# Part A's attention as one running line of steps: a step's sums grouped by tile shape and placed among the next step's scores, block ends deferred

## The chip, the cores and the metric

The kernel runs on one NeuronCore of a Trainium2 chip. Five engines work side by side, each through its own instructions in order: TensorE (PE, the matmul array, which writes to PSUM), VectorE (DVE), ScalarE (ACT), GpSimd (POOL) and SyncE (SP, which issues transfers). They meet through semaphores. The metric is the device time of one execution in microseconds (us); lower is better.

## What is computed

The reference is the forward pass and all gradients of a gated mix of two attentions over 2048 tokens of width 576. Only attention A is touched by the change; it has 32 query heads of width 18 that share one key head and one value head:

```
q = (x @ wq).reshape(B, S, H, Dh)          # H = 32, Dh = 18
k = x @ wk
v = x @ wv
scores = einsum('bhqd,bkd->bhqk', q, k) * Dh ** (-0.5)
p = softmax(scores)
a = einsum('bhqk,bkd->bhqd', p, v) @ wo
_out, _vjp = jax.vjp(_f, A_x, A_wq, ...)   # _f: g * a + (1 - g) * b
_grads = _vjp(grad_out)
```

Its backward pass needs, for each head, the exponentials E of the scores, the products of grad_out with v (called d here), U = d * E, and sums of E and of U over keys (for the output and dq) and over queries (for dk and dv).

## The kernel before

The program goes through attention A (set-up, attention, final products) and then through the stages of attention B. `a_attention` is the part of interest. It loops over 8 groups g of 4 heads. The 4 heads of a group lie at partitions 0, 32, 64 and 96 of one tile.

A group has two parts. **Part 0** keeps keys on the partitions: for each block of 512 queries (4 blocks) it goes over the 16 key tiles, and sums over keys into two PSUM tiles `a_acc0` and `a_acc1`. **Part 1** keeps queries on the partitions: for each block of 512 keys it goes over the 16 query tiles and sums over queries. That makes 8 x 2 x 4 x 16 = 1024 steps. One step is:

- twice `pair`, for two heads each: two score matmuls into `a_s` (all 128 rows and 128 columns of the array; the masked keys `a_kmask` pick the head), two exponentials on ScalarE from `a_s` into `a_E`, two matmuls into `a_d` that use 32 rows each of the array, and one VectorE product `a_U` = `a_d` * `a_E` over both heads;
- four sums of E: in part 0 with `a_evA` or `a_evB` as weights, 64 columns of the array each, in part 1 with `a_dog`, 32 columns each;
- four sums of U: with `a_ku` in part 0 and `a_qtok` in part 1, 32 columns each.

PSUM is full: two one-bank buffers for `a_s`, two two-bank buffers for `a_d`, one bank for each `a_acc`. `a_s` is free again when its exponential has read it, `a_d` when its product has.

After each part 0 block ScalarE and VectorE copy `a_acc` to `a_accs`, TensorE transposes that (eight f32 transposes into an `a_d` buffer), ScalarE copies it to `a_tk`, and VectorE and GpSimd form the output, dq and the normalised gradient in `a_dog`. After each part 1 block VectorE adds `a_acc` to `a_dvacc` and `a_dkacc`. At the start of a group and between its parts `tr16` makes the transposed `a_qtok`, `a_doT` and `a_doaT`, eight transposes to an `a_d` buffer, with a copy on VectorE or ScalarE in turn (`evac`).

The order on each engine is not the order of the code: the tile framework schedules the instructions by its own priorities. On TensorE it mixes the matmuls of neighbouring steps. The loads of a group are issued by SP (`a_qaug`) and by POOL (`a_dog`).

Of the kernel before, what the change touches and what calls it, by code (L numbers as in the profile page):

```python
# [7 lines left out]
ALU = mybir.AluOpType  # L8
AX = mybir.AxisListType
# [20 lines left out]
class Kern:  # L30
# [3 lines left out]
    def __init__(self, tc, T, A_x, A_wq, A_wk, A_wv, A_wo, B_mem0, B_Wq, B_Wk, B_Wv, B_Wo,  # L34
# [18 lines left out]
        self._evac_i = 0  # L53

# [9 lines left out]

    def mm(self, out, lhsT, rhs, start=True, stop=True, tp=None):
        return self.nc.tensor.matmul(out, lhsT, rhs, start=start, stop=stop,  # L66
                                     tile_position=tp, skip_group_check=True)

    def tr(self, out, in_, nrows, tp=None):
        b = in_.base_partition()  # L70
        return self.nc.tensor.transpose(out, in_, self.identB[b:b + nrows, b:b + nrows], tile_position=tp)  # L71
# [1014 lines left out]
    def a_attention(self, keep, sp, pacc, ps):  # L1086


        nc = self.nc
        T, NTT = self.T, self.NTT  # L1090
        self.otok = keep.tile([P, NTT, D], BF16, name="a_otok")
# [3 lines left out]

        def tr16(src_fn, dst):
            for t4 in range(0, NTT, 8):
                pt = ps.tile([P, 8, P], BF16, name="a_d", bufs=2)
                for t in range(8):
                    self.tr(pt[:, t, :], src_fn(t4 + t), P)  # L1100
                self.evac(dst[:, t4 * P:(t4 + 8) * P], pt[:].rearrange("p t c -> p (t c)"))

        srows = [slice(32 * i, 32 * i + 32) for i in range(4)]
        kmask = keep.tile([P, 4, T], BF16, name="a_kmask")
        nc.gpsimd.memset(kmask[:], 0.0)
        for i in range(4):
            nc.vector.tensor_copy(kmask[srows[i], i, :], self.kaug[srows[i], :])  # L1107

        def pair(pr, sl, sr, dl, dr):

            d = ps.tile([P, 2, 512], F32, name="a_d", bufs=2)
            ex = sp.tile([P, 2, 512], BF16, name="a_E", bufs=4)
            for j in range(2):
                s = ps.tile([P, 512], F32, name="a_s", bufs=2)
                self.mm(s[:, :], lhsT=sl(2 * pr + j), rhs=sr(2 * pr + j))
                nc.scalar.activation(ex[:, j, :], s[:, :], ACT.Exp, scale=SCALEA)  # L1116
            for j in range(2):
                r = srows[2 * pr + j]
                self.mm(d[:, j, :], lhsT=dl(r), rhs=dr(r), tp=(r.start, 0))
            u = sp.tile([P, 2, 512], BF16, name="a_U", bufs=4)  # L1120
            nc.vector.tensor_tensor(out=u[:], in0=d[:], in1=ex[:], op=ALU.mult)  # L1121
            return ex, u

        for g in range(8):
# [3 lines left out]
            nc.gpsimd.dma_start(dog[:, :, :], self.do_dram[g])  # L1128
            qtok = sp.tile([P, NTT * P], BF16, name="a_qtok", bufs=1)
            tr16(lambda t: qaug[:, t * P:(t + 1) * P], qtok)  # L1130
            doT = sp.tile([P, T], BF16, name="a_doT", bufs=1)
            tr16(lambda t: dog[:, t, :], doT)
            for qb in range(T // 512):
                qs = slice(qb * 512, qb * 512 + 512)
                acc = [pacc.tile([P, 512], F32, name=f"a_acc{b}", bufs=1) for b in range(2)]
                for kt in range(NTT):
                    ks = slice(kt * P, (kt + 1) * P)
                    Es, Us = zip(*[pair(pr, lambda i: kmask[:, i, ks], lambda i: qaug[:, qs],
                                        lambda r: self.vaugT[r, ks], lambda r: doT[r, qs]) for pr in range(2)])
                    for pr in range(2):  # L1140
                        ev = self.evA if pr == 0 else self.evB
                        for j in range(2):
                            self.mm(acc[pr][64 * j:64 * j + 64, :], lhsT=ev[:, kt, :], rhs=Es[pr][:, j, :],
                                    start=(kt == 0), stop=False, tp=(0, 64 * j))
                    for pr in range(2):
                        for j in range(2):
                            b = 64 * j + (32 if pr == 0 else 0)
                            self.mm(acc[pr][b:b + 32, :], lhsT=self.ku[:, kt, :], rhs=Us[pr][:, j, :],
                                    start=False, stop=(kt == NTT - 1), tp=(0, b))
                accs = sp.tile([P, 2, 512], F32, name="a_accs", bufs=1)  # L1150
                nc.scalar.copy(accs[:, 0, :], acc[0][:, :])
                nc.vector.tensor_copy(accs[:, 1, :], acc[1][:, :])
                pt = ps.tile([P, 2, 4, P], F32, name="a_d", bufs=2)
                for b in range(2):
                    for t in range(4):
                        nc.tensor.transpose(pt[:, b, t, :], accs[:, b, t * P:(t + 1) * P], self.identF[:])
                tk = sp.tile([P, 2, 4, P], F32, name="a_tk", bufs=1)
                nc.scalar.copy(tk[:], pt[:])
                ts = slice(qb * 4, qb * 4 + 4)
                for b in range(2):  # L1160
                    v = tk[:, b].rearrange("p t (j c) -> p t j c", c=64)
                    o0, k1, k2, u0 = (0, 19, 32, 37) if b == 0 else (32, 51, 0, 5)
                    h0 = 4 * g + 2 * b
                    osl = self.otok[:, ts, h0 * DA:(h0 + 2) * DA].rearrange("p t (j e) -> p t j e", e=DA)
                    qsl = self.dqtok[:, ts, h0 * DA:(h0 + 2) * DA].rearrange("p t (j e) -> p t j e", e=DA)
                    dsl = dog[:, ts, 64 * b:64 * b + 64].rearrange("p t (j c) -> p t j c", c=32)
                    rl = sp.tile([P, 4, 2, 1], F32, name="a_rl", bufs=2)
                    nc.vector.reciprocal(rl[:], v[:, :, :, o0 + 18:o0 + 19])
                    nc.gpsimd.tensor_tensor(out=osl, in0=v[:, :, :, o0:o0 + DA], in1=rl[:].to_broadcast([P, 4, 2, DA]),
                                            op=ALU.mult)  # L1170
                    prod = sp.tile([P, 4, 2, DA], F32, name="a_prod", bufs=2)
                    nc.gpsimd.tensor_tensor(out=prod[:], in0=osl, in1=dsl[:, :, :, 0:DA], op=ALU.mult)
                    dd = sp.tile([P, 4, 2, 1], F32, name="a_dd", bufs=2)
                    nc.vector.tensor_reduce(out=dd[:], in_=prod[:], axis=AX.X, op=ALU.add)
                    m1 = sp.tile([P, 4, 2, DA], F32, name="a_m1", bufs=2)
                    nc.gpsimd.tensor_tensor(out=m1[:, :, :, 0:13], in0=v[:, :, :, k1:k1 + 13],
                                            in1=dd[:].to_broadcast([P, 4, 2, 13]), op=ALU.mult)
                    nc.gpsimd.tensor_tensor(out=m1[:, :, :, 13:18], in0=v[:, :, :, k2:k2 + 5],
                                            in1=dd[:].to_broadcast([P, 4, 2, 5]), op=ALU.mult)
                    nc.gpsimd.tensor_tensor(out=m1[:], in0=v[:, :, :, u0:u0 + DA], in1=m1[:], op=ALU.subtract)  # L1180
                    nc.gpsimd.tensor_tensor(out=dsl[:, :, :, 0:DA], in0=dsl[:, :, :, 0:DA],
                                            in1=rl[:].to_broadcast([P, 4, 2, DA]), op=ALU.mult)
                    nc.vector.scalar_tensor_tensor(out=dsl[:, :, :, DA:DA + 1].rearrange("p t j c -> p t (j c)"),
                                                   in0=dd[:].rearrange("p t j c -> p t (j c)"), scalar=-1.0,
                                                   in1=rl[:].rearrange("p t j c -> p t (j c)"),
                                                   op0=ALU.mult, op1=ALU.mult)
                    rls = sp.tile([P, 4, 2, 1], F32, name="a_rls", bufs=2)
                    nc.gpsimd.tensor_scalar(out=rls[:], in0=rl[:], scalar1=SCALEA, scalar2=None, op0=ALU.mult)
                    nc.gpsimd.tensor_tensor(out=qsl, in0=m1[:], in1=rls[:].to_broadcast([P, 4, 2, DA]), op=ALU.mult)
            doaT = sp.tile([P, T], BF16, name="a_doaT", bufs=1)  # L1190
            tr16(lambda t: dog[:, t, :], doaT)
            for kb in range(T // 512):
                ks = slice(kb * 512, kb * 512 + 512)
                acc = [pacc.tile([P, 512], F32, name=f"a_acc{b}", bufs=1) for b in range(2)]
                for qt in range(NTT):
                    qs = slice(qt * P, (qt + 1) * P)
                    Es, Us = zip(*[pair(pr, lambda i: qaug[:, qs], lambda i: kmask[:, i, ks],
# [227 lines left out]
```

## Time and profile before

| | |
|---|---|
| median of 3 runs | 10380.04 us (10369.47 to 10390.74) |
| profiled execution | 10379.87 us, its span 10378.1 us |
| mean granted TensorE clock | 0.918 |
| PE, DVE, ACT, POOL busy | 9786.8, 4400.1, 3878.9, 1258.1 us |
| first score matmul of the attention | at 188.8 us |
| last sum of the attention | at 3734.3 us |

The span is the time between the first and the last instruction that the profiler saw. PE is busy by the modelled ends of pipelined matmuls, so 94% busy doesn't mean that the array streams 94% of the time: what a matmul costs is read from the distance between starts. In rows of the timeline "x2" merges instructions of one form that overlap or follow at once; the second number is the time from the first start to the last end. A row of a group ends with its busy time, the mean ns of one, and the idle time of its engine just before, with what ended it.

### The profile page before, as it was taken

The page shows a single profiled execution, that of the slowest core. Times are in us where ns is not written, and L with a number is a line of the kernel's source. Part 1 is how long each engine was busy: PE and PEld are TensorE (multiplying, and loading weights), DVE is VectorE, ACT ScalarE, POOL GpSimd, SP SyncE. Part 2 cuts the span into 40 slices and gives each one's busy share as a digit, 9 for nine tenths or more (in the row PEclk, how much of TensorE's full clock was granted, in tenths as well). Part 3 has the DMA queues.
Part 4 walks back from the last instruction along what each step waited for, and adds up shares of the span by engine and source line. Part 5 has one row for each costly group of instructions (what it writes and reads, how often), then busy time and mean ns, then how long its engine had stood idle before and what let it go on. Part 6 is the DMA issues. An engine that isn't in the chain of part 4 may idle for free. (4 is left out here: it accounts for less than half of the span.)

```text
span 10378.1 us, 211015 instructions
## 1 busy us (share of the span) xinstructions
PE 9786.8 (94%) x91222; PEld 4483.1 (43%) x91222; DVE 4400.1 (42%) x6058; ACT 3878.9 (37%) x6906; POOL 1258.1 (12%) x2895
## 2 busy tenths in 40 slices
PE   7999999999999989979999888888799989999899
PEld 2222222222222234435555555555566664555444
DVE  4777777777777744422222333333222221112100
ACT  3667676666766643321121222222111111112100
POOL 3000000000000003310000222322000001112100
PEclk9999999999999999979999877777899997777899
DMA  2000000000000025541111444444422236666644
GB/s 75 1 5 1 5 5 1 5 1 5 5 1 1 1 80 228 235 159 51 49 50 50 168 156 160 159 158 150 147 82 78 77 103 207 187 186 187 199 149 141
DMA packets 550264, 961.40 MB, mean 93 GB/s; under 512 B 183433, under 2 KB 361746, under 8 KB 529170
## 3 DMA queue, kind: packets, MB, share of 16 engines
q1 hardware_dynamic: 482850, 693.21, 20.9%
q0 software_dynamic: 65168, 253.37, 6.5%
q8 instruction: 713, 11.68, 0.5%
q14 instruction: 221, 1.81, 0.1%
q10 hardware_dynamic: 1312, 1.33, 0.0%
HBM read 543.67 MB, written 404.03 MB: 91 GB/s over the span
## 5 line engine op out<-in xcount | busy, mean ns | idle before, releaser
L1121 DVE TENSOR_TENSOR a_U<-a_d,a_E 128x1024 bf16<-128x1024 f32 x2048 | 2498.0, 1224 | 851.0 <-PE a_d L66 367.5
L1116 ACT ACTIVATE a_E<-a_s 128x512 bf16<-128x512 f32 x4096 | 2369.8, 597 | 1075.4 <-PE a_s L66 919.6
L66 PE MATMUL a_s<-a_qaug,a_kmask 128*128 128x512 bf16 x2048 | 783.3, 392 | 3.2 <-DVE a_kmask L1107 2.0
L66 PE MATMUL a_s<-a_kmask,a_qaug 128*128 128x512 bf16 x2048 | 719.3, 387 | 1.5
L66 PE MATMUL a_acc<-a_E,a_dog 128*32 128x512 bf16 x2048 | 583.3, 387 | 0.5
L66 PE MATMUL w_acc<-w_col,w_h 128*128 128x512 bf16 (+1 forms) x2400 | 526.1, 381 | 10.9 <-DMA w_col<-dqx 10.9
L66 PEld LDWEIGHTS <-d_g 128*32 128x32 bf16 x18432 | 498.5, 97 | 27.4 <-DVE d_g L728 10.1
L66 PEld LDWEIGHTS <-a_kmask 128*128 128x128 bf16 x2048 | 183.5, 96 | 567.5 <-issue 564.2
L66 PE MATMUL a_d<-a_doT,a_vaugT 32*128 32x512 bf16 x2048 | 409.5, 388 | 3.3 <-ACT a_doT L63 2.4
L66 PE MATMUL a_acc<-a_U,a_ku 128*32 128x512 bf16 x2048 | 405.9, 393 | 4.2 <-DVE a_U L1121 4.1
L66 PE MATMUL a_d<-a_vaugT,a_doaT 32*128 32x512 bf16 x2048 | 400.5, 384 | 4.9 <-DVE a_U L1121 4.9
L66 PE MATMUL a_acc<-a_U,a_qtok 128*32 128x512 bf16 x2048 | 402.3, 389 | 1.2 <-DVE a_U L1121 1.2
L61 DVE CAST p_tok<-p_pb 128x512 bf16<-128x512 f32 x384 | 265.3, 692 | 318.5 <-PE p_pb L66 318.5
L66 PE MATMUL a_acc<-a_E,a_evA 128*64 128x512 bf16 x1024 | 377.4, 407 | 0.0
L66 PE MATMUL a_acc<-a_E,a_evB 128*64 128x512 bf16 x1024 | 361.0, 396 | 10.4
L66 PEld LDWEIGHTS <-w_h 128*128 128x128 bf16 (+1 forms) x2400 | 237.4, 100 | 299.7 <-issue 34.3
L63 ACT COPY p_em<-p_tr 128x512 bf16<-128x512 bf16 x384 | 224.7, 585 | 358.2 <-PE p_tr L71 357.9
L66 PEld LDWEIGHTS <-a_qaug 128*128 128x128 bf16 x2048 | 158.4, 96 | 381.6 <-issue 381.6
L63 ACT CAST c_tm<-c_pb 128x512 bf16<-128x512 f32 x192 | 112.3, 585 | 543.1 <-PE c_pb L66 543.1
L66 PEld LDWEIGHTS <-c_mT 128*32 128x32 bf16 (+1 forms) x7680 | 166.8, 94 | 330.6 <-issue 211.7
L66 PEld LDWEIGHTS <-a_dog 128*32 128x32 bf16 x2048 | 134.4, 93 | 403.3 <-issue 403.3
L812 ACT ACTIVATE g_dt<-x_p 128x512 bf16<-128x512 f32 x256 | 142.8, 600 | 359.3 <-DMA dvx<-g_dt 210.0
(484 smaller groups left out, 14587.5 us busy)
## 6 DMA issues: line engine op xcount, KB each, us to landing
xt_k<-p_tok SPq DMA_DIRECT2D x16, 1024.0 KB, 3.9
xe_k<-p_em POOLq DMA_DIRECT2D x16, 1024.0 KB, 5.3
xs_k<-p_seg POOLq DMA_DIRECT2D x64, 256.0 KB, 3.7
xt_v<-p_tok SPq DMA_DIRECT2D x16, 1024.0 KB, 4.3
xe_v<-p_em POOLq DMA_DIRECT2D x16, 1024.0 KB, 5.9
xs_v<-p_seg POOLq DMA_DIRECT2D x64, 256.0 KB, 3.7
xt_q<-p_tok SPq DMA_DIRECT2D x16, 1024.0 KB, 4.6
xe_q<-p_em POOLq DMA_DIRECT2D x16, 1024.0 KB, 5.9
```

The costliest lines, as they stand in the source:

```text
L61: nc.vector.tensor_copy(out, in_)
L63: nc.scalar.copy(out, in_)
L66: return self.nc.tensor.matmul(out, lhsT, rhs, start=start, stop=stop, tile_position=tp, skip_group_check=True)
L812: nc.scalar.mul(dt[:, g], pk[:], sc)
L1116: nc.scalar.activation(ex[:, j, :], s[:, :], ACT.Exp, scale=SCALEA)
L1121: nc.vector.tensor_tensor(out=u[:], in0=d[:], in1=ex[:], op=ALU.mult)
```

## The change

`a_attention` becomes one line of 1024 steps over all groups and both parts. A step issues the scores and `a_d` of its first pair, then the four sums of E of the **previous** step, then its second pair, then the four sums of U of the previous step. `follow` ties every matmul and transpose of this line to the one before it, so TensorE keeps the order of the code. The work at the end of a block is split up and put at the end of later steps (`later`, `run_due`): the output work of a pair of heads one and two steps after the block's end (`outputs`), and the transposes in pieces of four (`tr4`), 3 steps apart for `a_qtok` and `a_doT`, and 8 steps after a block for `a_doaT`. All transposes now go through `a_s` buffers, where they went through `a_d`. A group's `a_qaug` and `a_dog` are both loaded by SP, at the second block of part 1 of the group before. `a_U` has 6 buffers, where it had 4. The matmuls, exponentials and products are the same in number and shape; the copies of transposes are twice as many at half the size.

```
+    def follow(self, ins):
+        ins = getattr(ins, "ins", ins)
+        if self.chain:
+            if self.last is not None:
+                self.tc.add_manual_dep(ins, self.last.name, mybir.DependencyInfo(
+                    mybir.DependencyClass.NoSync, mybir.DependencyReason.DATA), reason="order")
+            self.last = ins
...
-            u = sp.tile([P, 2, 512], BF16, name="a_U", bufs=4)
+            u = sp.tile([P, 2, 512], BF16, name="a_U", bufs=6)
...
+        def tr4(src_fn, dst, n):
+            pt = ps.tile([P, 4, P], BF16, name="a_s", bufs=2)
+            for t in range(4):
+                self.tr(pt[:, t, :], src_fn(4 * n + t), P)
+            self.evac(dst[:, blk(n, 512)], pt[:].rearrange("p t c -> p (t c)"))
...
+        def e_part(G, part, n, acc, Es):
+            st, sp_ = n == 0, n == NTT - 1
+            for i in range(4):
+                if part == 0:
+                    pr, j = i // 2, i % 2
+                    self.mm(acc[pr][64 * j:64 * j + 64, :], lhsT=(self.evA, self.evB)[pr][:, n, :], rhs=Es[pr][:, j, :],
+                            start=st, stop=False, tp=(0, 64 * j))
+                else:
+                    self.mm(acc[0][rows[i], :], lhsT=G["dog"][:, n, rows[i]], rhs=Es[i // 2][:, i % 2, :],
+                            start=st, stop=sp_, tp=(0, 32 * i))
...
+        def finish(G, part, b, acc, step):
+            if part == 1:
+                for src, dst in ((acc[0], self.dvacc), (acc[1], self.dkacc)):
...
+                        nc.vector.tensor_tensor(out=dst[:, blk(b, 512)], in0=dst[:, blk(b, 512)], in1=src[:, :], op=ALU.add)
+                return
+            accs = sp.tile([P, 2, 512], F32, name="a_accs", bufs=1)
+            nc.scalar.copy(accs[:, 0, :], acc[0][:, :])
+            nc.vector.tensor_copy(accs[:, 1, :], acc[1][:, :])
+            for pr in range(2):
+                later(step + 1 + pr, lambda pr=pr: outputs(G, b, pr, accs))
+            later(step + 8, lambda: tr4(lambda t: G["dog"][:, t, :], G["doaT"], b))
+        def outputs(G, qb, b, accs):
+            pt = ps.tile([P, 4, P], F32, name="a_s", bufs=2)
+            for t in range(4):
+                nc_tr = nc.tensor.transpose(pt[:, t, :], accs[:, b, blk(t, P)], self.identF[:])
+                self.follow(nc_tr)
+            tk = sp.tile([P, 4, P], F32, name="a_tk", bufs=2)
+            nc.scalar.copy(tk[:], pt[:])
...
+                        p0 = pair(0, *ops)
+                        if pending:
+                            e_part(*pending[0:4], pending[5])
+                        p1 = pair(1, *ops)
+                        if pending:
+                            u_part(*pending[0:4], pending[6])
+                            if pending[2] == NTT - 1:
+                                finish(pending[0], pending[1], pending[4], pending[3], step)
+                        run_due(step)
```

The order of instructions moves most on TensorE. In the middle of a part 0 block of the first group, where each row pair is a weight load and its matmul and the matmul's shape is rows of the output x elements, there stood before:

```order
L66 LDWEIGHTS a_kmask
L66 MATMUL a_s<-a_qaug,a_kmask 128x512
L66 LDWEIGHTS a_vaugT
L66 MATMUL a_d<-a_doT,a_vaugT 128x512
L66 LDWEIGHTS a_vaugT
L66 MATMUL a_d<-a_doT,a_vaugT 128x512
L66 LDWEIGHTS a_evA
L66 MATMUL a_acc_3947<-a_E,a_evA 64x512
L66 LDWEIGHTS a_evB
L66 MATMUL a_acc_3948<-a_E,a_evB 64x512
L66 LDWEIGHTS a_evB
L66 MATMUL a_acc_3948<-a_E,a_evB 64x512
```

and in the changed kernel, from the d of a step's first pair to the first score of its second:

```order
L78 LDWEIGHTS a_vaugT
L78 MATMUL a_d<-a_doT,a_vaugT 128x512
L78 LDWEIGHTS a_evA
L78 MATMUL a_acc_3920<-a_E,a_evA 64x512
L78 LDWEIGHTS a_evA
L78 MATMUL a_acc_3920<-a_E,a_evA 64x512
L78 LDWEIGHTS a_evB
L78 MATMUL a_acc_3921<-a_E,a_evB 64x512
L78 LDWEIGHTS a_evB
L78 MATMUL a_acc_3921<-a_E,a_evB 64x512
L78 LDWEIGHTS a_kmask
L78 MATMUL a_s<-a_qaug,a_kmask 128x512
```

The four sums of E, which stood apart in ones, twos and threes, now stand together; so do two scores, two d, and four sums of U.

On VectorE around the end of a part 0 block (the copy of an accumulator, then the output work of its two pairs) there stood before:

```order
L1152 COPY a_accs<-a_acc_2828 128x512
L1121 TENSOR_TENSOR a_U<-a_d,a_E 128x1024
L1168 RECIPROCAL a_rl<-a_tk 128x8 x2
L1121 TENSOR_TENSOR a_U<-a_d,a_E 128x1024
L1174 TENSOR_REDUCE a_dd<-a_prod 128x8 x2
```

and now:

```order
L1192 COPY a_accs<-a_acc_2783 128x512
L1128 TENSOR_TENSOR a_U<-a_d,a_E 128x1024 x3
L1214 RECIPROCAL a_rl<-a_tk 128x8
L1128 TENSOR_TENSOR a_U<-a_d,a_E 128x1024
L1220 TENSOR_REDUCE a_dd<-a_prod 128x8
L1229 SCALAR_TENSOR_TENSOR a_dog<-a_dd,a_rl 128x4x2
L1128 TENSOR_TENSOR a_U<-a_d,a_E 128x1024
L1214 RECIPROCAL a_rl<-a_tk 128x8
L1220 TENSOR_REDUCE a_dd<-a_prod 128x8
```

The two pairs' output work comes one after the other, a step apart, and the second pair's reduction follows its reciprocal with no product between them.

On ScalarE at the same ends there stood before:

```order
L1116 ACTIVATE a_E<-a_s 128x512 x62
L1151 COPY a_accs<-a_acc_3387 128x512
L1116 ACTIVATE a_E<-a_s 128x512 x2
L1158 COPY a_tk<-a_d 128x1024
```

and now:

```order
L1123 ACTIVATE a_E<-a_s 128x512 x56
L1191 COPY a_accs<-a_acc_2782 128x512
L1123 ACTIVATE a_E<-a_s 128x512 x4
L1205 COPY a_tk<-a_s 128x512
L1123 ACTIVATE a_E<-a_s 128x512 x4
L1205 COPY a_tk<-a_s 128x512
L1123 ACTIVATE a_E<-a_s 128x512 x24
L64 COPY a_doaT<-a_s 128x512
```

One copy of 1024 elements from an `a_d` buffer became two of 512 from `a_s` buffers, each behind a step's four exponentials, and a copy of a `tr4` follows six steps later.

More of the change, by code (lines that the diff above doesn't have):

```diff
@@ L1094, in a_attention @@
         self.dvacc = keep.tile([P, T], F32, name="a_dvacc")
[L1096 to L1103, printed above, removed]
+        rows = [slice(32 * i, 32 * i + 32) for i in range(4)]
         kmask = keep.tile([P, 4, T], BF16, name="a_kmask")
```

190 lines of the change are left out of this document (105 added, 85 removed).

## The prediction

> **What bounds the kernel now.** I read the page first (slices, costliest groups), then the tiles of the attention, then the timeline of TensorE inside a block. The slices show where the change can act; the two tile rows give the first score and the last sum.
>
> ```profile
> PE   7999999999999989979999888888799989999899
> ...
> L1121 DVE TENSOR_TENSOR a_U<-a_d,a_E 128x1024 bf16<-128x1024 f32 x2048 | 2498.0, 1224 | 851.0 <-PE a_d L66 367.5
> L1116 ACT ACTIVATE a_E<-a_s 128x512 bf16<-128x512 f32 x4096 | 2369.8, 597 | 1075.4 <-PE a_s L66 919.6
> ...
> L66 PE MATMUL a_s<-a_qaug,a_kmask x2048: 376/390/634, 188.8 to 3525.0; 128*128 128x512 bf16 x187
> ...
> L66 PE MATMUL a_acc<-a_U,a_qtok x2048: 376/390/391, 433.9 to 3734.3; 128*32 128x512 bf16 x187
> ```
>
> The attention runs from 188.8 to 3734.3: 3545.5 us for 1024 steps. TensorE has no idle time there, while VectorE and ScalarE sit idle 851 and 1075 us before their main work and wait for TensorE. So TensorE sets the pace. What it spends it on shows inside a step of part 1 (columns: start, time, engine, operation, how many together):
>
> ```profile
> 1500.02 0.39 PE L66 MATMUL a_s<-a_kmask,a_qaug 128*128 128x512 bf16 x1
> 1500.34 0.44 PE L66 MATMUL a_acc<-a_E,a_dog 128*32 128x512 bf16 x2
> 1500.71 0.39 PE L66 MATMUL a_s<-a_kmask,a_qaug 128*128 128x512 bf16 x1
> 1501.03 0.39 PE L66 MATMUL a_acc<-a_U,a_qtok 128*32 128x512 bf16 x2
> 1501.35 0.39 PE L66 MATMUL a_d<-a_vaugT,a_doaT 32*128 32x512 bf16 x2
> 1501.67 0.39 PE L66 MATMUL a_acc<-a_E,a_dog 128*32 128x512 bf16 x1
> 1501.99 0.61 PE L66 MATMUL a_s<-a_kmask,a_qaug 128*128 128x512 bf16 x2
> 1502.53 0.39 PE L66 MATMUL a_acc<-a_E,a_dog 128*32 128x512 bf16 x1
> ...
> 1502.86 0.39 PE L66 MATMUL a_d<-a_vaugT,a_doaT 32*128 32x512 bf16 x2
> 1503.17 0.39 PE L66 MATMUL a_s<-a_kmask,a_qaug 128*128 128x512 bf16 x1
> ...
> 783.78 0.39 PE L66 MATMUL a_acc<-a_U,a_ku 128*32 128x512 bf16 x2
> ...
> 787.43 0.39 PE L66 MATMUL a_acc<-a_U,a_ku 128*32 128x512 bf16 x2
> ```
>
> A step lasts 1503.17 - 1500.02 = 3.15 us in part 1 and, by the last two rows, 787.43 - 783.78 = 3.65 in part 0. Whatever the group holds, the next group of another shape starts 0.32 to 0.37 later; two scores in a row take 0.61, so the second starts 0.61 - 0.39 = 0.22 after the first. A group thus costs 0.22 of streaming and some 0.10 for the change of shape, and matmuls of one shape in different columns or rows of the array cost one stream. Nine groups make the 3.15. All steps together: 512 x 3.15 + 512 x 3.65 = 3482 of the 3545.5, so block ends cost 64 us now, hidden by the scheduler's mixing.
>
> **The change, steady steps.** It adds no matmul; it regroups them. The prices of the new groups are these rows:
>
> ```profile
> 808.78 0.41 PE L66 MATMUL a_acc<-a_E,a_evA 128*64 128x512 bf16 x2
> 809.02 0.38 PE L66 MATMUL a_acc<-a_E,a_evB 128*64 128x512 bf16 x1
> ...
> 867.68 0.40 PE L66 MATMUL a_acc<-a_E,a_dog 128*32 128x512 bf16 x3
> 868.01 0.39 PE L66 MATMUL a_s<-a_kmask,a_qaug 128*128 128x512 bf16 x1
> ```
>
> Two scores 0.54 (1501.99 to 1502.53), two d 0.32, sums of U 0.32, sums of E 0.33 in part 1 (three start together and the next shape follows 0.33 later; I take the same for four, in four columns). In part 0 two sums fill the 128 columns, so four take 0.24 + 0.31 = 0.55. TensorE alone: 0.54 + 0.32 + 0.33 + 0.54 + 0.32 + 0.32 = 2.37 in part 1, 2.59 in part 0.
>
> But the order is now fixed, and a score needs a free `a_s` buffer. The second score of a pair takes the buffer that the second exponential of the pair before must have read:
>
> ```profile
> 1502.42 2.47 ACT L1116 ACTIVATE a_E<-a_s 128x512 bf16<-128x512 f32 x4 [0.69 <-PE a_s L66]
> ...
> 806.01 0.81 PE L66 MATMUL a_s<-a_qaug,a_kmask 128*128 128x512 bf16 x2
> ...
> 805.79 0.60 ACT L1116 ACTIVATE a_E<-a_s 128x512 bf16<-128x512 f32 x1 [0.79 <-PE a_s L66]
> 806.28 0.58 ACT L1151 COPY a_accs<-a_acc 128x512 f32<-128x512 f32 x1
> ...
> 922.99 3.48 DVE L1121 TENSOR_TENSOR a_U<-a_d,a_E 128x1024 bf16<-128x1024 f32 x3
> ```
>
> A score at 1501.99 lets its exponential start at 1502.42: 0.43. ScalarE starts instructions 0.49 apart when they are ready (805.79, 806.28), each lasting 0.60. The second score of the row at 806.01 starts at 806.01 + 0.81 - 0.38 = 806.44, and the exponential that it waited for ended at 806.39: 0.05. So from a pair's first score to the next pair's second at least 0.43 + 0.49 + 0.60 + 0.05 = 1.57 pass. From there TensorE needs score to d 0.32, d 0.32 and the sums to reach the next pair's first score. With sums of 0.32 that loop is 1.57 + 0.96 = 2.53; it binds part 1, just above its 2.37. In part 0, the loop through the pair followed by the sums of E is 1.57 + 0.32 + 0.32 + 0.55 = 2.76. VectorE's products follow each other in (3.48 - 1.23) / 2 = 1.13, 2.26 a step: close, but not the bound. I take 2.53 and 2.76: 512 x 2.53 + 512 x 2.76 = 2708. The floor is TensorE's own sum, 512 x (2.37 + 2.59) = 2540; the other end is no gain, 3482.
>
> **The change, block ends.** With the order fixed, what the scheduler hid stands on the line. The prices:
>
> ```profile
> 807.97 0.66 PE L1156 MATMUL a_d<-identF,a_accs 128*128 128x128 f32 x4
> 808.47 0.38 PE L66 MATMUL a_s<-a_qaug,a_kmask 128*128 128x512 bf16 x1
> ...
> 808.72 1.01 ACT L1158 COPY a_tk<-a_d 128x1024 f32<-128x1024 f32 x1 [0.87 <-PE a_d L1156]
> ...
> 868.32 0.38 PE L71 MATMUL a_d<-identB,a_dog 128*128 128x128 bf16 x4
> ...
> 866.02 0.69 DVE L1152 COPY a_accs<-a_acc 128x512 f32<-128x512 f32 x1 [0.92 <-PE a_acc L66]
> 867.58 0.69 DVE L61 COPY a_doaT<-a_d 128x1024 bf16<-128x1024 bf16 x1 [0.86 <-PE a_d L71]
> ...
> 870.30 0.69 DVE L1174 TENSOR_REDUCE a_dd<-a_prod 128x8 f32<-128x144 f32 x2 [1.46 <-POOL a_prod L1172]
> ...
> a_dog<-do_dram POOLq DMA_DIRECT2D x8, 512.0 KB, 3.7
> ```
>
> - *Accumulator, 64 ends.* A block's last sums come at the end of the next block's first step, and the new block's first sums of E one pair later; they need `a_acc` read. VectorE reads it only after that step's second product, which waits for the step's last exponential. In part 1 the second pair's first score is at 0.54 + 0.32 + 0.33 = 1.19, its exponentials end 1.52 later at 2.71, and the product starts at about 2.77, 0.25 after the step's end at 2.53 (part 0: at 3.15, 0.4 after 2.76). Product 1.13 + read 0.69 (the row at 866.02) + 0.05 puts the sums at 2.1 behind the step's end, due at 0.54 + 0.32 = 0.9: 1.2 late, of which the usual wait hides 0.1. In part 0 the `evB` sums come at 2.3, due at 1.25: 1.0. That is 32 x 1.1 + 32 x 1.0 = 67 us. Queued behind the waiting sums are the next scores, so both other engines run dry.
> - *Output transposes, 64.* Four take 0.50 (807.97 to 808.47). They hold an `a_s` buffer until ScalarE has copied it; the copy starts 0.36 after the last transpose (808.47 - 0.11 to 808.72) and takes 0.58 (its half-size like the row at 806.28). The step's second score starts at 0.50 - 0.11 + 0.36 + 0.58 + 0.05 = 1.38, where it usually starts at 0.38: 64 x 1.0 = 64.
> - *Output work on VectorE, 32.* The second reduction waits for GpSimd's two products behind the reciprocal; for two pairs at once that idle time was 1.46, for one, between that and nothing, I take 1.0, less 0.3 of slack: 0.7, 22 us in all.
> - *`tr4`, 92 behind the start.* Four bf16 transposes start 0.06 apart (0.38 for the row of 868.32). With the copy on ScalarE the second score comes at 0.22 + 0.24 + 0.58 + 0.05 = 1.1: 0.7 late. On VectorE the copy stands behind the second product: 0.4 + 1.13 + 0.4 (0.69 for twice the size) = 1.9, so 1.5 late. Half of each: 92 x 1.1 = 101.
>
> Without cover lost elsewhere the line is 2708 + 67 + 64 + 22 + 101 = 2962 us. The loads moved to SP are issued 8 steps, some 20 us, ahead of first use, land in 3.7, and SP's queue holds nothing else between them: nothing. The extra `a_U` buffers: nothing. The other stages keep their order: nothing.
>
> **The clock.** The new stalls leave TensorE idle in one piece, and the windows of before show what that does (PE, PEld, DVE, ACT, POOL busy with counts, granted clock, DMA share, GB/s):
>
> ```profile
> 1959.00:1962.40 3.40, 2.30 (x13) 0.78 (x12) 2.86 (x4) 2.04 (x3) 0.00 (x0) 1.00 0.00 0
> 1962.40:1972.60 10.20, 10.20 (x33) 1.91 (x32) 5.71 (x5) 4.09 (x8) 0.00 (x0) 0.50 0.00 0
> ...
> 3290.20:3317.50 27.30, 27.30 (x85) 5.12 (x83) 14.01 (x12) 10.10 (x19) 0.00 (x0) 0.50 0.00 1
> ...
> 1518.60:1522.00 3.40, 2.50 (x14) 0.78 (x13) 3.38 (x3) 2.03 (x5) 0.00 (x0) 1.00 0.02 5
> ...
> 1964.24 0.61 PE L66 MATMUL a_s<-a_qaug,a_kmask 128*128 128x512 bf16 x1
> 1964.78 0.61 PE L66 MATMUL a_acc<-a_U,a_ku 128*32 128x512 bf16 x2
> ```
>
> A stretch of 3.4 us with PE busy 2.30 was followed by 10 us at a granted clock of 0.50; one with 2.50 was not. At 0.50 a group takes 0.54 in place of 0.32, a new step some 4.1 to 4.5 in place of 2.53 to 2.76, so each 3.4 us there lose 3.4 x 0.38 = 1.3. The gaps of the part 1 ends (32, idle about 1.15, busy 2.25) and of `tr4` on VectorE (46, idle about 1.4, busy 2.0) lie below 2.30 where one such stretch holds the whole gap, about 6 of 10. The return should be quicker than before, since more of the line streams at 0.50 (3.4 of 4.1 against 0.43 of 0.54): one or two stretches, 1.9 us. 78 x 0.6 x 1.9 = 89; bounds 0 and the rivals below.
>
> The Trainium skill ("TensorE: Matmul & The Clock Gate", "HAM oscillation — how this bites in real kernels") puts the rule at no idle gaps above about 3.4 us. By it no gap here would halve the clock, and the sum would lose its 89 us. The trace does not agree: the stretch of 1959.00 had 1.10 us idle in all, and the clock fell.
>
> **The sum.** 2962 + 89 = 3051 against 3545.5: 494.5 less. The profiled execution took 10379.87 us (0.2 from the median), so 10379.9 - 494.5 = 9885.
>
> **The rivals.**
> - *The clock doesn't fall.* The two windows leave the bound between 2.30 and 2.50 busy, and my gaps are computed, not seen. Then 10379.9 - 3545.5 + 2962 = 9796. The page on the clock gate named above would have this.
> - *The clock falls at most of the 78 gaps and stays down three stretches,* as at 1962.40: 3.9 us each, 183 (6 of 10) to 304: 9980 to 10100.
> - *Slower: the clock stays down.* Place: the same 78 gaps. Price: 27.3 us at 0.50, as at 3290.20, lose 10.4 each, 811 in all: 10607. It decides the sign from (10380 - 9796) / 78 = 7.5 us per gap, 20 us at 0.50. Against it: the denser line.
> - *Four columns don't run as one.* If only two did, both sums of part 1 and those of U in part 0 cost 0.22 more each: 512 x 0.44 + 512 x 0.22 = 338 on 9885, less what the exponentials hid: about 10180. Against it: three together at 867.68.
> - *The ends cost less.* If half of the 254 us of ends and the clock's 89 hide: about 9715.
> - *The order isn't kept or the shape change isn't the cost:* 10380. Against: nine groups of 0.32 make the step.
>
> **How the numbers follow.** Forecast 0.45; clock stays up 0.17; three stretches 0.17; slower 0.06; two columns only 0.06; ends hidden 0.05; no effect 0.04. The likeliest gives 9885. The range reaches from 9770 (clock up, ends a little cheaper) to 10080 (most of the three-stretch case). Faster by over 0.2% (about what can be told from no change here): 0.90; within: 0.04; slower: 0.06.
>
> **What would show it.** Steps of 2.53 and 2.76 between equal scores inside blocks; groups of two scores, two d and four sums that start together; second scores that start 0.05 behind an exponential. At ends: sums of E behind the VectorE read, and second scores behind `a_tk` and `tr4` copies. Windows at 0.50 after them. Wrong would be: steps near 3 us (columns not together), VectorE without idle time (it would be the bound), or a mean clock in the attention far below 0.95.

## The result and the profile after

| | before | after |
|---|---|---|
| median of 4 runs each | 10383.56 us (10369.47 to 10390.74) | 9746.86 us (9740.96 to 9752.44) |
| ratio, 95% interval | 1 | 0.9388 [0.9372, 0.9405] |
| profiled execution | 10379.87 us, span 10378.1 | 9740.96 us, span 9738.9 |
| first score to last sum of the attention | 3545.5 us | 2897.0 us |
| the rest of the span | 6832.6 us | 6841.9 us |
| a step inside a block, part 0 / part 1 | 3.65 / 3.15 us | 2.74 / 2.52 us |

The change makes the kernel 6.1% faster. The forecast was 9885 with a range from 9770 to 10080: the direction was right and the gain was larger than forecast, with a median 23 us below the range's low end. All of the gain lies in the attention: 3545.5 - 2897.0 = 648.5 us; the rest of the span took 9 us more, inside the 6833 to 6852 us that it took over all the profiled runs.

The page and the tile rows of the changed kernel that answer to those of before: the slices with the clock, the two main groups (busy, mean ns, idle before, releaser), the first score and the last sum.

```profile
PE   7999999999999898899998888887999989998899
...
PEclk9999999999999899899997777777999987776999
...
L1128 DVE TENSOR_TENSOR a_U<-a_d,a_E 128x1024 bf16<-128x1024 f32 x2048 | 2472.6, 1223 | 295.2 <-ACT a_E L1123 224.0
L1123 ACT ACTIVATE a_E<-a_s 128x512 bf16<-128x512 f32 x4096 | 2237.7, 595 | 556.7 <-PE a_s L78 471.8
```

```profile
L78 PE MATMUL a_s<-a_qaug,a_kmask x2048: 376/379/634, 189.7 to 2913.2; 128*128 128x512 bf16 x187
...
L78 PE MATMUL a_acc<-a_U,a_qtok x2048: 376/390/610, 387.4 to 3086.7; 128*32 128x512 bf16 x187
```

The idle time of VectorE ahead of its products fell from 851 to 295 us, and the largest part of it is no longer put down to TensorE's d but to ScalarE's exponentials; ScalarE's own idle time halved. The three engines now share one loop. The whole attention as one window (busy and count of PE, PEld, DVE, ACT, POOL, then clock, DMA share, GB/s), of before and then of after:

```profile
188.80:3734.30 3545.50, 3517.68 (x17008) 1003.73 (x17008) 2610.71 (x2357) 2434.22 (x4187) 181.65 (x520) 0.99 0.01 3
```

```profile
189.00:3087.00 2898.00, 2780.66 (x17010) 710.55 (x17008) 2570.41 (x2382) 2303.90 (x4243) 185.77 (x512) 0.99 0.01 3
```

The matmuls are the same 17008 (two more by the window's edges); PE's busy time is 737 us less. What was taken out is not work of the other engines, which are busy nearly as long as before, but time between matmuls. The timeline of TensorE inside a part 0 block and then inside a part 1 block shows the new step:

```profile
964.07 0.75 PE L78 MATMUL a_s<-a_qaug,a_kmask 128*128 128x512 bf16 x2
964.76 0.39 PE L78 MATMUL a_d<-a_doT,a_vaugT 32*128 32x512 bf16 x2
965.07 0.41 PE L78 MATMUL a_acc<-a_E,a_evA 128*64 128x512 bf16 x2
965.31 0.38 PE L78 MATMUL a_acc<-a_E,a_evB 128*64 128x512 bf16 x2
965.63 0.60 PE L78 MATMUL a_s<-a_qaug,a_kmask 128*128 128x512 bf16 x2
966.17 0.39 PE L78 MATMUL a_d<-a_doT,a_vaugT 32*128 32x512 bf16 x2
966.48 0.40 PE L78 MATMUL a_acc<-a_U,a_ku 128*32 128x512 bf16 x4
966.82 0.75 PE L78 MATMUL a_s<-a_qaug,a_kmask 128*128 128x512 bf16 x2
...
1204.80 0.75 PE L78 MATMUL a_s<-a_kmask,a_qaug 128*128 128x512 bf16 x2
...
1205.80 0.40 PE L78 MATMUL a_acc<-a_E,a_dog 128*32 128x512 bf16 x4
1206.13 0.60 PE L78 MATMUL a_s<-a_kmask,a_qaug 128*128 128x512 bf16 x2
...
1207.32 0.39 PE L78 MATMUL a_s<-a_kmask,a_qaug 128*128 128x512 bf16 x1
```

A step takes 966.82 - 964.07 = 2.75 us in part 0 and 1207.32 - 1204.80 = 2.52 in part 1. Four sums in four columns last 0.40 together and the next shape starts 0.33 later: they run as one. The two scores ahead of d last 0.75 in place of 0.60, which is the wait for the `a_s` buffer: the second starts 0.37 after the first and not 0.22. Over all steps the medians are 2.745 and 2.523, taken from the distance of every fourth exponential.

### The profile page after: what moved, and what is told of

Its sections match the earlier page's. It is cut to its first block, busy times and chain, and to the rows that moved or that the text cites. A ratio compares the mean times of both kernels' runs of the same rounds, so it can differ in the third digit from the quotient of the medians.

```text
span 9738.9 us, 211095 instructions
## 1 busy us (share of the span) xinstructions
PE 9052.5 (93%) x91222; PEld 4192.6 (43%) x91222; DVE 4369.3 (45%) x6082; ACT 3748.2 (38%) x6962; POOL 1261.4 (13%) x2887
## 5 line engine op out<-in xcount | busy, mean ns | idle before, releaser
L1128 DVE TENSOR_TENSOR a_U<-a_d,a_E 128x1024 bf16<-128x1024 f32 x2048 | 2472.6, 1223 | 295.2 <-ACT a_E L1123 224.0
L1123 ACT ACTIVATE a_E<-a_s 128x512 bf16<-128x512 f32 x4096 | 2237.7, 595 | 556.7 <-PE a_s L78 471.8
L78 PE MATMUL a_s<-a_qaug,a_kmask 128*128 128x512 bf16 x2048 | 700.1, 385 | 54.7 <-ACT a_tk L1205 24.5
L1215 POOL TENSOR_TENSOR a_otok<-a_tk,a_rl 128x144 bf16<-128x144 f32 x64 | 27.4, 428 | 2514.1 <-DVE a_rl L1214 2514.1
L78 PEld LDWEIGHTS <-a_vaugT 32*128 32x128 bf16 x2048 | 96.1, 91 | 569.0 <-issue 569.0
L78 PEld LDWEIGHTS <-a_doaT 32*128 32x128 bf16 x2048 | 96.3, 91 | 537.9 <-issue 537.5
L62 DVE CAST w_o<-w_acc 128x512 bf16<-128x512 f32 (+1 forms) x60 | 41.4, 690 | 491.7 <-PE w_acc L78 475.4
L78 PEld LDWEIGHTS <-a_kmask 128*128 128x128 bf16 x2048 | 124.9, 97 | 311.2 <-issue 303.1
L78 PEld LDWEIGHTS <-p_xT 128*128 128x128 bf16 (+1 forms) x1920 | 155.0, 97 | 218.4 <-issue 88.4
L78 PE MATMUL x_b<-WTq,g_dqe 128*128 128x512 bf16 (+1 forms) x1024 | 200.7, 360 | 42.9 <-DMA g_dqe<-dqe 42.9
```

What stands on the lines that cost most here:

```text
L62: nc.vector.tensor_copy(out, in_)
L78: self.follow(self.nc.tensor.matmul(out, lhsT, rhs, start=start, stop=stop, tile_position=tp, skip_group_check=True))
```

## The experiments

Each experiment is an edit of the changed kernel, shown shortened, with "..." or words for what is left out; two of them hold the edit of another, as is said there. The theory was the prediction's: the steady step is the loop through the exponentials and the `a_s` buffers; what made it possible is fewer changes of shape on TensorE; block ends are stalls that stand on the line; the clock falls where a stall is long. "Attention" is first score to last sum of the profiled execution, and "at 0.50" is the time in it that the trace's clock records show there. Every attention here also starts at 0.50 and stays there for its first 5 to 33 us; that is not counted. Each ratio is to runs of before that were taken with it, whose medians were 10376.8 to 10383.6 us.

| kernel | median us | ratio to before [95%] | attention us | at 0.50 us |
|---|---|---|---|---|
| after | 9746.9 | 0.9388 [0.9372, 0.9405] | 2897.0 | 17.1 |
| sums together | 9954.4 | 0.959 [0.9571, 0.9609] | 3112.3 | 0 |
| ungrouped | 10984.1 | 1.0582 [1.0559, 1.0604] | 4113.1 | 1631.6 |
| ungrouped, ends moved | 10333.7 | 0.996 [0.9941, 0.998] | 3465.1 | 99.0 |
| free order | 10147.7 | 0.9777 [0.9758, 0.9797] | 3303.4 | 0 |
| copy late | 9778.1 | 0.942 [0.9406, 0.9434] | 2930.2 | 41 |
| ends at once | 9781.0 | 0.9425 [0.941, 0.9439] | 2928.5 | 44.4 |
| `tr4` copies on ScalarE | 9754.3 | 0.9398 [0.9382, 0.9414] | 2902.1 | 78.5 |
| ends moved | 9689.2 | 0.9338 [0.9324, 0.9352] | 2848.8 | 17.1 |
| longer gap | 9843.3 | 0.9481 [0.9465, 0.9497] | 3003.5 | 262.8 |

### What sets the step

**Sums together.** The sums of E move from between the two pairs to behind the second; the shapes stay grouped.

```
  p0 = pair(0, *ops)
- if pending: e_part(...)
  p1 = pair(1, *ops)
+ if pending: e_part(...)
  if pending: u_part(...)
```

> All eight sums of the previous step stand together behind the step's second pair; the matmuls are the same, and part 1 has one change of shape less per step. Theory of the prediction (a_s buffers and exponentials set the pace): from the first score of a pair to the second score of the next at least 1.57 us, then d, d and all sums, so a step takes about 1.57 + 0.64 + 0.54 = 2.75 in part 1 (2.52 in the changed kernel) and 1.57 + 0.64 + 0.87 = 3.08 in part 0 (2.74): 118 + 174 us more, less some 30 at the part 1 ends, where the sums come later: about 10010. Rival (only the number of shape changes counts): part 1 steps 0.1 shorter, part 0 the same: about 9695.

```profile
1500.35 0.60 PE L78 MATMUL a_s<-a_qaug,a_kmask 128*128 128x512 bf16 x2
1500.88 0.39 PE L78 MATMUL a_d<-a_doT,a_vaugT 32*128 32x512 bf16 x2
1501.42 0.86 PE L78 MATMUL a_s<-a_qaug,a_kmask 128*128 128x512 bf16 x2
...
1503.42 0.39 PE L78 MATMUL a_s<-a_qaug,a_kmask 128*128 128x512 bf16 x1
```

On TensorE's timeline of this kernel the second pair's scores now start 0.54 behind d and last 0.86: both wait for an exponential. The steps are 1503.42 - 1500.35 = 3.07 in part 0 and 2.74 in part 1, where the loop gave 3.08 and 2.75. So a step can hold no more changes of shape than the changed kernel's and still be 0.22 to 0.33 longer: **the `a_s` loop sets the step, and the sums between the pairs are what fills it.** The time was 56 us below the expected one. By the medians over all steps, 3.074 and 2.737, the steps account for 14 us of that. Most of the rest is that the ends cost less than supposed (0.06 per part 1 end), and that the clock never fell behind the start, though TensorE idles more here in sum: no single idle piece there is above 0.72 us.

**Ungrouped.** The sums of two heads each stand between the scores; ten groups per step.

```
- e_part(...)                # four heads, between the pairs
+ p0 = pair(0, *ops, mid=E of heads 0, 1)   # mid: between its two scores
+ E of heads 2, 3
+ p1 = pair(1, *ops, mid=U of heads 0, 1)
+ U of heads 2, 3
```

> Fixed order, previous step's sums and deferred ends stay; only the grouping by shape goes: score, two sums of E, score, two d, two sums of E, score, two sums of U, score, two d, two sums of U, ten groups of one shape. Theory (changes of shape cost 0.10 each and TensorE sets the pace): ten groups of 0.32 to 0.33, steps of 3.2 to 3.25 in both parts, 512 x 0.7 + 512 x 0.5 = 610 us more: about 10360. Rival (the gain comes from the pipelining by a step and the deferred ends): within 100 us of the changed kernel's 9747.

The steps at full clock were 3.25 in part 0 and 3.22 in part 1, as ten groups of 0.32 give. But the time missed by 620 us. The whole attention of this kernel, and TensorE's timeline in one part 1 block:

```profile
188.00:4301.00 4113.00, 4038.05 (x17008) 1069.14 (x17007) 2610.90 (x2380) 2509.67 (x4242) 186.03 (x512) 0.80 0.01 2
```

```profile
1500.31 0.61 PE L78 MATMUL a_s<-a_kmask,a_qaug 128*128 128x512 bf16 x1
1500.84 0.61 PE L78 MATMUL a_acc<-a_U,a_qtok 128*32 128x512 bf16 x2
...
1505.71 0.61 PE L78 MATMUL a_s<-a_kmask,a_qaug 128*128 128x512 bf16 x1
```

The mean granted clock was 0.80. In the rows, which lie in one of 15 episodes at 0.50, groups cost 0.54 and a step 1505.71 - 1500.31 = 5.40. The longest episode lasted 263 us (its last 9 lie behind the attention). All 15 follow a stretch that holds the gap of a part 1 end, here 1.58 us, or 1.40 of it and more. This is the mechanism of the prediction's slower rival: the clock falls at an end and stays down for long. It does so here, in a line whose array streams less of the time than the changed kernel's.

**Ungrouped, ends moved.** To have the grouping's price without the clock, the same order with the edit of "ends moved" (below), which takes the first addition of the part 1 ends (groups 1 to 7) and all `tr4` copies off VectorE.

> e3_ungrouped with the ends of e8_ends_moved: ten groups of one shape per step, but no wait of the sums of E for VectorE at the part 1 ends of groups 1 to 7. Theory (e3's 10984 are 610 us of shape changes and some 620 us of lowered clock, which fell at the part 1 ends and couldn't return in so thinly streaming a line): steps of 3.22 and 3.25 in nearly all blocks, some 614 us over e8's 9689: 10300, with under 250 us at a granted clock of 0.5 in the attention (1632 in e3). Rival (the ungrouped line lowers the clock by itself): 10900, with over 1000 us at 0.5.

```profile
1500.07 0.39 PE L78 MATMUL a_s<-a_kmask,a_qaug 128*128 128x512 bf16 x1
...
1503.29 0.39 PE L78 MATMUL a_s<-a_kmask,a_qaug 128*128 128x512 bf16 x1
```

At the same place the step takes 1503.29 - 1500.07 = 3.22, ten groups. One episode at 0.50 is left, behind an end of the first group, whose ends the edit does not touch. Two things follow. The stalls at the part 1 ends are what sent "ungrouped" to 0.50. And beside "ends moved", which differs only in the order of the matmuls inside a step, the attention is 3465.1 - 2848.8 = 616 us longer and the median 645 (about 33 us of this may come from 82 us more at 0.50, where a step of 5.40 in place of 3.22 loses 0.40 of each): **grouping by shape is worth about as much as the whole gain.** The running line, the deferred ends and even the moved ends together, without the grouping, come out at 0.996 of before.

**Free order.** `follow` ties nothing, so the scheduler is free on TensorE again.

```
- self.chain = True
+ self.chain = False
```

> The code order of the changed kernel, but TensorE's instructions aren't tied to each other, so the framework's scheduler places them. It changes shape 8.7 times per step on TensorE, where the changed kernel does so 6.1 times and the kernel before 9.5 times. Theory (each group of one shape costs 0.32, TensorE sets the pace): steps near 3.0 us, 250 to 400 us more than the changed kernel: 10000 to 10150. Rival (the deferred ends and the pipelined code make the gain, and the tie adds nothing): 9747, within 30.

```profile
1504.24 0.40 PE L78 MATMUL a_acc<-a_U,a_ku 128*32 128x512 bf16 x4
1504.57 0.40 PE L78 MATMUL a_acc<-a_E,a_evA 128*64 128x512 bf16 x1
1504.90 0.39 PE L78 MATMUL a_s<-a_qaug,a_kmask 128*128 128x512 bf16 x1
1505.22 0.40 PE L78 MATMUL a_acc<-a_E,a_evA 128*64 128x512 bf16 x1
```

The four sums of U still stand together, the sums of E come apart, and a lone score stands between them. Steps in part 1 rise to 3.43. The time is at the upper end of the expected span. Writing the groups in the code is not enough; the tie keeps them, and is worth 400 us.

### What the block ends cost

After's timeline shows the three kinds of end. First VectorE at the end of a part 0 block, then TensorE and VectorE at the end of a part 1 block:

```profile
964.43 2.41 DVE L1128 TENSOR_TENSOR a_U<-a_d,a_E 128x1024 bf16<-128x1024 f32 x2 [0.33 <-ACT a_E L1123]
966.96 0.69 DVE L1192 COPY a_accs<-a_acc 128x512 f32<-128x512 f32 x1
967.57 3.57 DVE L1128 TENSOR_TENSOR a_U<-a_d,a_E 128x1024 bf16<-128x1024 f32 x3
...
1195.99 0.39 PE L78 MATMUL a_d<-a_vaugT,a_doaT 32*128 32x512 bf16 x2
1197.53 0.40 PE L78 MATMUL a_acc<-a_E,a_dog 128*32 128x512 bf16 x4 [1.16 <-DVE a_dvacc L1188]
...
1194.33 2.56 DVE L1128 TENSOR_TENSOR a_U<-a_d,a_E 128x1024 bf16<-128x1024 f32 x2
1196.80 0.68 DVE L1188 TENSOR_TENSOR a_dvacc<-a_dvacc,a_acc 128x512 f32<-128x512 f32 x1
```

In part 1 the sums of E wait 1.16 us for the read of `a_acc`, which stands behind both products, as forecast; the end costs 1.23. In part 0 the copy at 966.96 stands **ahead** of the second product, and that end costs 0.25. The third kind, a `tr4` with its copy on VectorE (rows of TensorE, then ScalarE, then VectorE):

```profile
810.94 0.40 PE L83 MATMUL a_s<-identB,a_dog 128*128 128x128 bf16 x4
811.31 0.38 PE L78 MATMUL a_s<-a_kmask,a_qaug 128*128 128x512 bf16 x1
812.37 0.38 PE L78 MATMUL a_s<-a_kmask,a_qaug 128*128 128x512 bf16 x1 [0.69 <-ACT a_E L1123]
...
811.73 0.60 ACT L1123 ACTIVATE a_E<-a_s 128x512 bf16<-128x512 f32 x1 [0.46 <-PE a_s L78]
...
812.43 0.41 DVE L62 COPY a_doT<-a_s 128x512 bf16<-128x512 bf16 x1
```

The second score starts at 812.37, before the copy of the transposes has even begun: it took the buffer of the first score, free when the exponential ended at 812.33, and not the transposes' own. The end costs 1.06.

**Copy late.** The VectorE copy of the part 0 end is kept behind the step's second product, where the prediction had it.

```
- nc.vector.tensor_copy(accs[:, 1, :], acc[1][:, :])
+ cp = nc.vector.tensor_copy(accs[:, 1, :], acc[1][:, :])
+ self.tc.add_manual_dep(cp, lastU, NoSync)      # order only
```

> The VectorE copy of the accumulator at a part 0 end is kept behind the second product of its step, as the prediction had placed it; in the changed kernel it stands ahead of that product. Theory (the order on VectorE explains why part 0 ends cost less than predicted): sums of E wait about 0.75 us more at each of 32 ends, 24 us more: about 9771. Rival (it doesn't matter where the copy stands): 9747.

```profile
970.77 0.41 PE L78 MATMUL a_acc<-a_E,a_evB 128*64 128x512 bf16 x2 [0.82 <-DVE a_accs L1192]
```

TensorE now waits 0.82 us for the copy; the end's second step takes 4.31 in place of 3.36. This wait stands at 24 of the 32 ends: behind the last block of a group's part 0 the next sums are those of part 1, and that step is as long as before. 24 x 0.96 = 23 us, and 24 us more at 0.50 lose about 9 by the prediction's rate; the attention is 33 us longer. So at those ends the prediction's price of 1.0 was about right for the order that it assumed; the kernel has the other order.

**Ends at once.** `outputs` runs at the block's last step for both pairs, not one and two steps later.

```
- later(step + 1 + pr, lambda pr=pr: outputs(G, b, pr, accs))
+ later(step, lambda pr=pr: outputs(G, b, pr, accs))
```

> The output work of both pairs follows a part 0 block's end in the same step; everything else stays. Theory (deferring hides the wait for the accumulator copies): TensorE waits about 0.9 us for them, and both a_s buffers are held by transposes at once: 1.2 to 1.5 us more at 32 ends, 40 to 50 us, and with such gaps the clock falls at some of them: 9790 to 9870. Rival (the deferral is worth nothing): 9747.

```profile
969.79 1.09 PE L1202 MATMUL a_s<-identF,a_accs 128*128 128x128 f32 x8 [0.79 <-ACT a_accs L1191]
971.17 0.86 PE L78 MATMUL a_s<-a_qaug,a_kmask 128*128 128x512 bf16 x2 [0.29 <-ACT a_tk L1205]
```

The transposes wait 0.79 for ScalarE's copy of the accumulator. Deferral saves 32 us of attention and 34 of the median. By the step lengths an end costs 0.72 to 0.78 us more, about half of what was expected, 24 us for 32; the 27 us more at 0.50 lose about 10 by the prediction's rate. The row shows why the end costs less: the transposes of both pairs, side by side, share one wait.

**`tr4` copies on ScalarE.** All copies of `tr4` go to ScalarE, where one costs 0.69 by after's trace, not 1.06.

```
- self.evac(dst[:, blk(n, 512)], ...)
+ self.evac(dst[:, blk(n, 512)], ..., use="s")
```

> All copies of the pieces of four transposes go to ScalarE, where half of them went to VectorE. By the step lengths of the changed kernel a piece costs 1.06 us with VectorE and 0.69 with ScalarE. Theory (a piece costs what the next second score waits for its a_s buffer): 46 x 0.37 = 17 us less: 9730. Rival (ScalarE's exponentials lose as much as VectorE gains): 9747 or more.

Each piece now costs 0.69 to 0.70, as expected, but the time shows no difference to the changed kernel (the intervals overlap). The attention held 78.5 us at 0.50, 41 us of it in one episode, against 17.1. The 61 us more at 0.50 lose about 61 x 0.38 = 23 by the prediction's rate, more than the 17 us that the shorter stalls save. One trace alone shows these episodes, but the mean granted clock of the four runs agrees: 0.907 to 0.911 over the span, against 0.912 to 0.913 in the changed kernel's four.

**Ends moved.** Together with the edit before, ScalarE copies the first accumulator of a part 1 end to SBUF and GpSimd adds it; VectorE adds the second alone (groups 1 to 7).

```
+ elif src is acc[0]:
+     x = sp.tile([P, 512], F32, name="a_x", bufs=2)
+     nc.scalar.copy(x[:, :], src[:, :])
+     nc.gpsimd.tensor_tensor(out=dst[:, blk(b, 512)], in0=dst[:, blk(b, 512)], in1=x[:, :], op=ALU.add)
```

> As e6_tr4_act, and at 28 part 1 ends ScalarE copies the first accumulator to SBUF right behind the step's exponentials and GpSimd adds it there, so the next sums of E no longer wait for VectorE behind the second product. Theory (the end's 1.23 us is that wait): some 0.3 remains for ScalarE's copy, 28 x 0.9 = 25 us less, and no stretch at a granted clock of 0.5 follows a part 1 end, 6 us less: with e6's 17 about 9700. Rival (ScalarE becomes late with its exponentials, or GpSimd's addition holds the copy's buffer): no gain over e6, 9730 or more.

```profile
1184.42 0.40 PE L78 MATMUL a_acc<-a_U,a_qtok 128*32 128x512 bf16 x4
1184.82 0.86 PE L78 MATMUL a_s<-a_kmask,a_qaug 128*128 128x512 bf16 x2
1185.62 0.39 PE L78 MATMUL a_d<-a_vaugT,a_doaT 32*128 32x512 bf16 x2
1185.94 0.40 PE L78 MATMUL a_acc<-a_E,a_dog 128*32 128x512 bf16 x4
```

TensorE runs through the end: the sums of E follow d after 0.32, and what is left is 0.07 ahead of the first score and 0.11 at the second, 0.18 per end in place of 1.23. 28 x 1.05 = 29 us, and 17 of the `tr4` copies, give 46; the attention is 48 shorter. Its 17.1 us at 0.50 lie at ends of the first group, which the edit leaves alone. This version is faster than both kernels: 9689.2, 0.9338 [0.9324, 0.9352] of before.

### When the clock falls

**Longer gap.** An extra read of the first accumulator (0.6 us on VectorE, its result unused) ahead of the part 1 end's addition.

```
+ if src is acc[0]:
+     x = sp.tile([P, 512], F32, name="a_x", bufs=1)
+     nc.vector.tensor_copy(x[:, :], src[:, :])
  nc.vector.tensor_tensor(out=dst[:, blk(b, 512)], ...)
```

> One more VectorE read of an accumulator (0.69 us, result unused) ahead of the addition at 28 part 1 ends. Theory (the clock falls when a stretch of 3.4 us streams less than some 0.43, and the gaps of the changed kernel end just at it): gaps some 0.6 longer, 17 us by themselves, and the clock falls at 12 to 20 of the ends for one or two stretches of 3.4 us, 15 to 50 us more: 9780 to 9815, and 50 us or more at a granted clock of 0.5 in the attention (17 in the changed kernel). Rival (gaps below some 3 us never lower the clock): 9764, with some 17 us at 0.5 as before.

```profile
187.00:3191.00 3004.00, 2871.65 (x17008) 715.37 (x17008) 2589.91 (x2408) 2304.18 (x4243) 185.78 (x512) 0.95 0.01 3
...
1172.54 0.40 PE L78 MATMUL a_acc<-a_E,a_dog 128*32 128x512 bf16 x4 [1.76 <-DVE a_dvacc L1191]
```

The direction is as expected and the size larger. 28 gaps of 0.6 are 17 us, yet the attention is 106 longer: 262.8 us ran at 0.50, in 27 episodes of 3.4 to 17.1 us, and the 246 us more than in the changed kernel lose about 93 by the prediction's rate. The rival that gaps under 3 us never lower the clock is out: the longest idle piece of TensorE here is 1.76 us, as in the second row.

In every trace the clock changes at times that lie multiples of 3.413 us apart, so stretches are cut there. Two of them in the changed kernel, each with a part 1 end's gap, then what followed the second, and two rows of TensorE in that one:

```profile
1960.70:1964.10 3.40, 2.24 (x16) 0.51 (x14) 3.29 (x4) 2.17 (x4) 0.00 (x0) 1.00 0.02 5
3042.80:3046.20 3.40, 2.24 (x16) 0.57 (x16) 3.29 (x5) 2.01 (x4) 0.00 (x0) 0.99 0.00 0
3046.20:3049.60 3.40, 3.40 (x16) 0.56 (x14) 2.33 (x2) 2.17 (x4) 0.00 (x0) 0.50 0.00 0
...
3047.86 1.04 PE L78 MATMUL a_s<-a_kmask,a_qaug 128*128 128x512 bf16 x2
3048.83 0.61 PE L78 MATMUL a_d<-a_vaugT,a_doaT 32*128 32x512 bf16 x2
```

Both are busy 2.24 us with 16 matmuls; the first was followed by full clock, the second by 0.50. Of 26 such stretches in the attention (busy 2.16 to 2.28) 22 were followed by full clock and 4 by 0.50. Counted in the same way over the attentions of all eleven traces, at full clock: each of the 55 stretches with PE busy below 2.20 us was followed by 0.50; of the 122 between 2.20 and 2.42 us 20 were; of the 9392 above, none. The gap of 1.16 us stands in this border, where what decides stays open, and 0.6 more is clearly past it.

## Why the prediction was right, and where it was wrong

| step of the prediction | forecast us | measured in after |
|---|---|---|
| steady steps, 2.76 and 2.53 | 2708 | 2697 (512 x 2.745 + 512 x 2.523) |
| accumulator, part 1 ends | 32 x 1.1 | 32 x 1.23 |
| accumulator, part 0 ends | 32 x 1.0 | 32 x 0.25 |
| output transposes | 64 x 1.0 | 32 x 1.82, for two |
| output work on VectorE | 32 x 0.7 | 0 |
| `tr4` | 46 x 0.7, 46 x 1.5 | 46 x 0.69, 46 x 1.06 |
| clock, 32 gaps of part 1 ends | 37 | about 7 |
| clock, 46 gaps of `tr4` on VectorE | 52 | 0 |
| the line | 3051 | 2897 |

**The steady step was right**, to 0.02 us, and for its reason: "sums together" moved the loop as computed. TensorE's own sum for a part 1 step, 2.37, was not reached; the buffers bind. That the gain comes from the changes of shape is shown by "ungrouped, ends moved".

**The step that failed is the clock: "78 x 0.6 x 1.9 = 89".** It took 78 gaps that leave PE busy below 2.30 us in a stretch, and the halved clock behind 6 of 10. Only 17.1 us ran at 0.50, about 7 us lost at the prediction's 1.3 per stretch: 82 of the 154 us that the line came out shorter. Two things in the term were wrong. For 46 of the gaps, those of `tr4` on VectorE, the wait itself was mis-sized: they were put at 1.4 us idle and 2.0 busy, but all 46 idle 0.69, as at 812.37, and the clock fell behind none of them. That is 52 of the 89 us, and it has the same origin as the price of `tr4` below. The 32 gaps of the part 1 ends were foreseen (idle about 1.15 against 1.16, busy 2.25 against 2.24), but 4 falls followed in place of 19: the bound of 2.30 was drawn from one stretch, and these gaps lie in the border in which the traces go both ways. The mechanism is real all the same: "longer gap" and "ungrouped" show it with 263 and 1632 us. By the time alone the nearest rival is "the ends cost less" (9715); by what happened it is "the clock doesn't fall" (9796), with ends that cost 68 us less as well.

The Trainium skill ("TensorE: Matmul & The Clock Gate", "HAM oscillation — how this bites in real kernels") has no idle gaps above about 3.4 us as its rule, and by it nothing would fall. For the changed kernel that came nearer than the prediction's sum. The runs contradict it as a bound: 1.76 us of idle was enough in "longer gap". Of the same page of the Trainium skill the next section, "A second HAM failure mode: psum-queue depth-cycling", tells of a clock that goes up and down because the array idles briefly and often between groups of matmuls; the falls here agree with that in so far as their idle pieces were short, at most 0.61 to 1.76 us.

**The ends, 254 forecast, came to 186, which is 68 us of the rest.** The mis-sized terms: the part 0 accumulator (24 us), because the prediction put the VectorE copy behind the second product, while in the order printed above the prediction three products follow the copy, the first of them that step's second; "copy late" confirms the price for the order that was assumed, at 24 of the 32 ends. `tr4` on VectorE (20 us), because the second score was taken to wait for the copy and takes another buffer instead; this is read from the trace, and the edit that moved the copies confirms only the price of the ScalarE kind. The reduction (22 us): VectorE does wait for GpSimd there and its products come late, but no step gets longer; this was read from the trace and not tried by itself. The steady steps were 11 us shorter than forecast, and about 8 us of the line, at its start and its end, are assigned to none of these.

**Nothing else moved.** The other stages show no difference in the rest of the span beyond its own scatter. In the changed kernel's trace no wait of TensorE in the attention is put down to a transfer, so the loads on SP cost nothing, as forecast. The extra `a_U` buffers were not tried by themselves.

## What to carry to other kernels

Look at the distance between starts on TensorE and not at its busy time: where neighbouring groups of different tile shape start 0.32 us apart for 0.22 of streaming, put matmuls of one shape together and tie the order, because a free scheduler takes the groups apart again. Then find the loop through the small PSUM pool that takes over as the bound, and fill its wait with work that is already due, one step late if need be. Where the line then has single stalls of a microsecond, shorten those first: by themselves they are small, but they can lower the clock, as those of 1.16 us did now and then here and those of 1.76 us nearly always.

## What the runs showed of the hardware

- The granted clock fell after idle pieces far shorter than a stretch of 3.4 us: with pieces of 1.16 us in 4 of 26 stretches of the changed kernel, with 1.76 for 263 us in all, and in the attention of before twice with no piece above 0.61. Idle time of 325 us in pieces of at most 0.72 ("sums together") did not lower it. What the falls have in common is PE's busy time in the stretch: in these eleven traces below 2.20 of 3.41 us always, above 2.42 never.
- The return went with how densely the line streams: the grouped lines came back after 3.4 to 17.1 us, once after 41; in the ungrouped one, whose groups stream 0.43 of each 0.54 us, 11 of 15 episodes lasted more than 50 us, the longest 263.
- A change of tile shape costs about the same time at either clock. At 0.50 two scores reach the next shape after 3048.83 - 3047.86 = 0.97 us and one group after 0.54, so a stream is 0.43 there, where it is 0.22 at full clock; groups of one stream start 0.54 and 0.32 apart, so a change is about 0.10 us each time.
- Four matmuls of 32 columns each start together and cost one stream: 0.33 us to the next shape, as for one.
